# An attention and MLP kernel: lending more dead SBUF as exp outputs and shift buffers, and a second shifted copy on GpSimd

## The chip, the core and the metric

The kernel runs on one core of a Trainium2 chip. The metric is device microseconds (us) from start to end of one execution of the whole program. Engines are named as in the profile: PE (TensorE, matmuls), ACT (ScalarE), DVE (VectorE), POOL (GpSimd), SP (the queue that issues all DMAs here).

## What is computed

Two layers of pre-norm attention and an MLP with GELU, in bfloat16, on one sequence of 2048 tokens of width 512, with 32 heads of 16 and a hidden width of 1792. Both layers share their weights.

```python
def _A_ref(x, wqkv, wo):                       # x: [1, 2048, 512]
    qkv = (x @ wqkv).reshape(B, S, 3, H, Dh)   # H = 32, Dh = 16
    scores = einsum("bhqd,bhkd->bhqk", q, k) * (Dh ** -0.5)
    o = einsum("bhqk,bhkd->bhqd", softmax(scores), v)
    return o.reshape(B, S, D) @ wo
def _B_ref(x, w1, b1, w2, b2):                 # F = 1792
    return gelu(x @ w1 + b1) @ w2 + b2
for _ in range(2):
    x = x + _A_ref(layernorm(x), wqkv, wo)
    x = x + _B_ref(layernorm(x), w1, b1, w2, b2)
```

## The kernel before

**Cells.** The unit of attention is a *cell*: the scores of one head for 128 keys and 512 queries, one matmul of K = 32 rows (L1244; the queries are masked to one head by POOL, L1192, into QP). There are 4096 cells. Queries come in segments of 512 (the last one in two of 256); a *pass* is one head pair of a segment, four cells for each block of 128 keys.

**Two ways to exp.** Most cells go to ACT: groups of two or three cells lie in neighbouring PSUM banks (a *slot*), one ACTIVATE (L1601) takes the exp of the group and writes bfloat16 into places of 512 columns, the `PT` pool. Each such cell needs one matmul with V (PV, L1665), four of which run side by side on column groups of PE.
The other way is the *shift path*. DVE turns the scores into 16-bit integers whose bits, read as bfloat16, are a coarse exp (`dfirst`, L1396). Then `dchain` (L1459 on) makes three shifted copies, for a pair of cells at once: POOL adds 32 (L1473: slice 1 from slice 0), DVE adds 64 to both (L1478: slices 2 and 3 from 0 and 1, 2048 elements). PV sums the four slices with V and three scaled copies of V (`VC`, made by POOL in `vcopies`), so such a cell needs four PV matmuls. The slices lie in a *shift buffer* (`DU`), which is held from the scoring of its first cell until PV has read its last slice. Only five of the sixteen key blocks of a layer may take this path (`KD`).

**Who chooses.** All instructions are laid out ahead by a planner (`_Sched`, and `_Plan` with its generators). Each generator yields operations with costs; the planner keeps a clock for each engine, always commits the operation that can start first, and writes out the order for each engine with the semaphore waits that the data need. When a score group is committed, `attach` (L1325) may add a shift cell in a spare bank, and else `swap` (L1302) gives the third bank of the group to a shift cell, so that ACT has two cells in place of three. Both need an open pair or a free shift buffer. Constants at the head of the file set these choices; `TOL` bounds how late a bank may be, `WARM` sets when the planner adds matmuls that do nothing but keep PE busy (`fill`, L1232). `_ready` also keeps operations marked `port` (DVE's shifts) from being planned while POOL runs.

**Memory that is lent.** While parts of K of layer 1, of Q, and of V of layer 0 hold nothing, their space is given to `PT` as more places (`lent`, `lent_q`, `lend_units`; the profile then names the output kt, q or v). Beside its own 15 places and five pair buffers, the kernel before lends one more pair buffer in dead K of layer 0 once layer 0's attention is over (`morebuf`). A region is taken back when its owner needs it.

**The rest.** `post` does a segment's output projection (`wo`, L881 adds it to x), layer norm (`ln`, `ln_tile`), the h matmuls (`hpair`, L976 adds the bias into `G`), GELU on ACT (L997), the second MLP matmul (`ytile`, L1029) and the projections of layer 1 (`proj`: K and Q at L756, V at L770), spread under the attention of the next segment. Layer norm takes statistics on DVE (L666, L668), adds epsilon (L671, DVE), takes the power -1/2 on POOL (L673), makes -mean x rstd (L676, DVE) and then x x rstd + that (L689, POOL; DVE for the four first tiles and the two last). The result goes through a transposing DMA from SP (L693) into XF or XP, which the planner books with `0.3` us of SP and a tail of 3.5.

Of the kernel before, what the change touches and what calls it, by code (L numbers as in the profile page):

```python
# [5 lines left out]
ALU = mybir.AluOpType  # L6
# [7 lines left out]
H = 32  # L14
# [4 lines left out]
NL = 2  # L19
# [32 lines left out]
TOL = 0.2  # L52
# [3 lines left out]
QUEUE = 4  # L56
RUSH = 4
WINDOW = 3.4
WARM = 2.3
# [14 lines left out]
PSHIFT = 3  # L74
# [111 lines left out]
class _Op:  # L186
    __slots__ = ("eng", "cost", "fns", "reads", "writes", "sem", "by", "tail", "prio", "mode", "slack", "late", "back", "port", "limit", "after")

    def __init__(self, eng, cost, fns, reads=(), writes=(), sem=None, by=1, tail=0.0, prio=None, mode="F", slack=None):
        self.eng, self.cost = eng, cost  # L190
        self.fns = fns if isinstance(fns, list) else [fns]
        self.reads, self.writes = list(reads), list(writes)
        self.sem, self.by, self.tail, self.prio, self.mode, self.slack = sem, by, tail, prio, mode, slack
        self.limit = 1e9
        self.late, self.after = None, []
        self.port = eng == "dve" and self.writes[:1] != [] and self.writes[0].startswith(("OTT", "NMR"))
# [13 lines left out]
OWN = 0.022  # L210
HEAD = 0.14
LATENCY = {"pe": 0.2175, "act": 0.21, "dve": 0.139, "pool": 0.153328, "sp": 0.1}
OVERLAP = 0.083
# [225 lines left out]
def bass_interleave_layers__mha_block__dense_activation_gelu__prompt_kernel(  # L439
# [15 lines left out]
    with ExitStack() as es:  # L455
# [22 lines left out]
        T["PT"].append(vf[0][:, 0:8192].rearrange("p (n q) -> p n q", q=512))  # L478
# [8 lines left out]
        T["DU"].append(late.rearrange("p (i j q) -> p i j q", i=4, j=2))  # L487
        T["VC"] = sb([128, NKD, 3, H * 17], BF16, "vc")
# [15 lines left out]
        T["NMR"] = sb([128, NT], F32, "nmr")  # L504
# [37 lines left out]
SLACK = 0.3  # L542
LATE = 0.7


class _Plan:
# [12 lines left out]
    def init(self):  # L559
        T, hbm = self.T, self.hbm  # L560

        def load(dst, src, sem, keys, cost):
# [17 lines left out]
        yield ("need", ("otn", 0, (0, 0, 512), 3))  # L580
        yield _Op("pool", 1.0, lambda e: e.memset(T["V"][1][:, :, :, 16:17], 1.0),
                  writes=["V11"] + ["PART.0.%d" % g for g in range(8)])
        yield ("give", "v1ones")
# [75 lines left out]
    def ln(self, tiles, dst, dkeys, prio, quick=False, gate=None):  # L659
# [4 lines left out]
        for t in tiles:  # L664
# [6 lines left out]
        yield _Op("dve", 0.16, lambda e: e.tensor_scalar(T["VARR"][:, sl], T["MV"][:, sl, 1], 1e-5, None, op0=ALU.add),  # L671
# [4 lines left out]
        yield _Op("dve", 0.157, lambda e: e.scalar_tensor_tensor(  # L676
            out=T["NMR"][:, sl], in0=T["MV"][:, sl, 0], scalar=-1.0, in1=T["RSTD"][:, sl], op0=ALU.mult, op1=ALU.mult),
            reads=mvk + ["RSTD.%d" % c], writes=["NMR.%d" % c])
# [5 lines left out]
    def ln_tile(self, c, t, dst, dkeys, quick):  # L684
# [5 lines left out]
            T["XLN"][:, x, :], T["X"][:, t % XT, :], T["RSTD"][:, t:t + 1], T["NMR"][:, t:t + 1], op0=ALU.mult, op1=ALU.add),  # L690
            reads=["X.%d" % (t % XT), "RSTD.%d" % c, "NMR.%d" % c], writes=["XLN.%d" % x])
        if not quick:
            yield _Op("sp", 0.3, lambda e: e.dma_start(dst(t), T["XLN"][:, x, :], transpose=True),  # L693
                      reads=["XLN.%d" % x], writes=dkeys(t), sem="dtr%d" % x, by=16, tail=3.5)
            yield ("rel", "xln", x)
            yield ("give", ("lnt", t, ph))
            return
# [14 lines left out]
    def proj(self, l, kind, i, c, src, skeys, ph, done):  # L712
# [44 lines left out]
        if kind == "K":  # L757
            keys = ["K%d.%d.%d" % (l, i, c)]
            if l == 1:
                keys += ["XL.%d" % t for t in range(4 * c, 4 * c + 4)]  # L760
                if c in LEND:
                    yield ("need", ("k1", c))
# [6 lines left out]
        else:  # L769
            yield _Op("dve", DV, lambda e: e.tensor_copy(T["V"][l][:, i, :, 0:16], pb.rearrange("p (h d) -> p h d", h=H)),  # L770
# [166 lines left out]
    def wlate(self, todo):  # L937
        over = ["K0.%d.%d" % (i, c) for i in (0, 1) for c in range(self.NQ)] + ["PART1.%d" % g for g in range(4)]
        for i, (piece, (src, n), uses) in enumerate(todo):
            yield from self.wload(piece, src, n, uses, W_RING + i, over)  # L940
# [105 lines left out]
    def post(self, l, seg):  # L1046
# [20 lines left out]
        if prev:  # L1067
            yield ("need", ("gfree",) + prev)
        for p in range(NFC // 2):
# [69 lines left out]
    def setup_attention(self):  # L1139
# [18 lines left out]
        self.cap = [2] * (DU // 2) + [1] * (DU % 2) + [2]  # L1158
# [8 lines left out]
    def vcopies(self):  # L1167
        T = self.T
        for l in range(NL):
            yield ("cond", lambda l=l: self.pv >= self.lead[l])  # L1170
            for j, kt in enumerate(KD[l]):
                yield ("need", ("V", l, kt, kt // 4))
                src = T["V"][l][:, kt, :, :].rearrange("p h c -> p (h c)")
                for i, w in enumerate(VW):
                    yield _Op("pool", 0.68, lambda e, j=j, i=i, w=w, src=src: e.tensor_scalar(
                        T["VC"][:, j, i, :], src, w, 1.0, op0=ALU.mult, op1=ALU.mult),
                        reads=["V%d.%d" % (l, kt), "V%d1" % l], writes=["VC.%d.%d" % (j, i)])
# [273 lines left out]
    def over(self, du):  # L1451
        return ["K0.%d.%d" % (i, c) for i in (2, 3) for c in range(self.NQ)] if du == len(self.cap) - 1 else []

    def morebuf(self):
        yield ("cond", lambda: self.pa >= self.lead[1])
        yield ("cond", lambda: all(x == 0 for x in self.left[:self.lead[1]]))
        yield ("rel", "du", len(self.cap) - 1)

    def dchain(self, pair):  # L1459
# [22 lines left out]
        yield two  # L1482
        self.duleft[du] = n
        for jj, (pi, kt, a) in enumerate(cells):
# [30 lines left out]
    def setup_units(self):  # L1515
# [12 lines left out]
        lo = self.blocks[-1][1]  # L1528
        self.blocks.append((lo, lo + 16))
# [53 lines left out]
    def exps(self):  # L1583
        T = self.T
        u = 0
        while True:
# [17 lines left out]
            for r, (pi, kt, a) in zip(run, cells):  # L1604
# [3 lines left out]
                                         ["V%d.%d" % (l, kt), "V%d1" % l] + self.pkeys(r), ("pt", r), True, kt))  # L1608
# [100 lines left out]
    def run(self):  # L1709
# [15 lines left out]
        s.pool("du", range(len(self.cap) - 1))  # L1725
# [9 lines left out]
        s.spawn(self.morebuf(), 4)  # L1735
        s.spawn(self.lend_units(), 4)
# [36 lines left out]
```

## Time and profile before

| | |
|---|---|
| median of 3 runs | 1520.87 us (1520.8, 1520.87, 1523.39) |
| span of the profiled execution, first to last instruction | 1522.5 us; no time of its own beside the span is given |
| busy: PE, DVE, ACT, POOL | 1449.7, 1333.5, 1477.5, 823.6 us |
| cells through ACT / through the shift path | 3051 / 1045 |
| exp groups of three cells / of two | 421 / 894 |
| L1473 (POOL) / L1478 (DVE), for a pair | 1.170 / 0.744 us mean, 1.044 / 0.684 median |

The span and the runs are the same measure up to a few tenths of a per cent, so the profile's durations can be set against the median. Busy time of PE is modelled with overlapping matmuls and contains matmuls that only keep it busy, so 95% is not a full PE. A row of the profile gives busy time, mean length in ns, and the engine's idle time just before such instructions, with what ended it. Lines are those of the kernel before.

### The profile page before, as it was taken

To read this page: it belongs to the slowest core of one execution; us is meant where nothing else is said; L and a number is where in the kernel's file an instruction comes from. 1 tells how busy PE (TensorE), PEld (TensorE's weight loads), DVE (VectorE), ACT (ScalarE), POOL (GpSimd) and SP (SyncE) were. 2 spreads that over 40 slices of the span, in tenths; PEclk is the share of its full clock that TensorE was granted. 3 is DMA by queue.
4 is the path that set the end of the run, shared out by engine and by line. 5 is a ranking of instruction groups with operands and counts; after the bars stand their busy time and mean duration, and the time that the engine had idled before them with its cause. 6 is when DMAs were issued, how large, how long until landed. Compare 5 with 4: busy or idle time off the path is not lost.

```text
span 1522.5 us, 46554 instructions
## 1 busy us (share of the span) xinstructions
PE 1449.7 (95%) x20337; PEld 446.0 (29%) x20337; DVE 1333.5 (88%) x2255; ACT 1477.5 (97%) x1374; POOL 823.6 (54%) x783
## 2 busy tenths in 40 slices
PE   8998889999999999999999999899999999999998
PEld 2222222222222222222222222222222222344445
DVE  6568888989999899889989889899989999999994
ACT  7999999999999999999999999999999999999995
POOL 5425545556465554646565466556556656564550
PEclk9999999999999999999999999999999999999999
DMA  5200001144121531125221351001143115412522
GB/s 150 47 2 2 2 2 43 29 126 119 29 57 37 153 92 42 37 62 165 62 57 29 91 141 56 15 2 36 43 139 99 36 29 151 124 37 69 157 68 78
DMA packets 145046, 103.40 MB, mean 68 GB/s; under 512 B 37069, under 2 KB 143822, under 8 KB 144846
## 3 DMA queue, kind: packets, MB, share of 16 engines
q1 hardware_dynamic: 144846, 100.44, 23.4%
q8 instruction: 162, 2.65, 0.7%
q14 instruction: 38, 0.31, 0.1%
HBM read 88.61 MB, written 4.19 MB: 61 GB/s over the span
## 4 chain that ended last, share of the span: by engine, by line
ACT 58%; PE 29%; DVE 10%; issue 1%; POOL 1%; DMA 0%; ACTq 0%; DVEq 0%
ACT pt L1601 47%; PE ps L556 10%; PE ps L1244 9%; PE ps L1665 9%; ACT kt L1601 4%; DVE du L1396 4%; ACT g L997 3%; ACT v L1601 2%; DVE du L1478 2%; ACT q L1601 1%; DVE kt L1396 1%; PE ps L1232 1%; DVE g L976 1%; ACT L1601 1%; ACT L997 1%
## 5 line engine op out<-in xcount | busy, mean ns | idle before, releaser
L1601 ACT ACTIVATE pt<-ps 128x1024 bf16<-128x1024 f32 (+1 forms) x1115 | 1195.5, 1213 | 13.5 <-PE ps L1244 9.2
L1473 POOL TENSOR_SCALAR du<-du 128x1024 uint16<-128x1024 uint16 x478 | 558.6, 1170 | 482.9 <-DVE du L1396 469.3
L1396 DVE TENSOR_SCALAR du<-ps 128x512 uint16<-128x512 f32 x955 | 635.6, 683 | 82.5 <-PE ps L1244 77.6
L1244 PE MATMUL ps<-qp,kt 32*128 32x512 bf16 x4096 | 532.0, 385 | 29.9 <-ACT pt L1601 18.1
L1665 PE MATMUL ps<-pt,v 128*17 128x512 bf16 (+1 forms) x2866 | 400.6, 361 | 11.5 <-ACT pt L1601 7.9
L1665 PE MATMUL ps<-du,vc 128*17 128x512 bf16 (+1 forms) x3213 | 372.9, 359 | 5.0 <-DVE du L1478 2.0
L1478 DVE TENSOR_SCALAR du<-du 128x2048 uint16<-128x2048 uint16 x478 | 350.5, 744 | 12.0 <-POOL du L1473 11.7
L1244 PEld LDWEIGHTS ps<-qp,kt 32*128 32x128 bf16 x4096 | 137.7, 91 | 570.0 <-ACT pt L1601 191.9
L1665 PE MATMUL ps<-du,v 128*17 128x512 bf16 (+1 forms) x1071 | 178.9, 360 | 8.0 <-ACT pt L1601 2.2
L1673 PE MATMUL ps<-vc,zero 128*17 128x512 bf16 x805 | 167.0, 381 | 0.0
L556 PE MATMUL ps<-xf,wr 128*32 128x512 bf16 (+1 forms) x1888 | 129.9, 366 | 2.6 <-DMA xf<-xln 1.3
L1665 PEld LDWEIGHTS ps<-pt,v 128*17 128x17 bf16 x2866 | 98.8, 88 | 108.7 <-issue 64.8
L1665 PEld LDWEIGHTS ps<-du,vc 128*17 128x17 bf16 x3213 | 102.3, 89 | 87.7 <-issue 46.0
L556 PE MATMUL ps<-wr,g 128*32 128x512 bf16 x1600 | 117.4, 382 | 1.9 <-DVE du L1396 1.4
L1192 POOL TENSOR_SCALAR qp<-q,mask 128x512 bf16<-128x512 bf16 (+1 forms) x91 | 76.1, 837 | 63.6 <-PE ps L1244 56.5
L1601 ACT ACTIVATE kt<-ps 128x1536 bf16<-128x1536 f32 (+1 forms) x81 | 102.0, 1268 | 5.0 <-PE ps L1244 3.6
L1473 POOL TENSOR_SCALAR kt<-kt 128x1024 uint16<-128x1024 uint16 x45 | 54.6, 1214 | 75.8 <-DVE kt L1396 74.2
L1601 ACT ACTIVATE v<-ps 128x1024 bf16<-128x1024 f32 (+1 forms) x74 | 85.6, 1187 | 2.7 <-PE ps L1244 1.1
L976 DVE TENSOR_SCALAR g<-ps,hb1t 128x512 bf16<-128x512 f32 (+1 forms) x112 | 79.1, 706 | 7.3 <-PE ps L556 7.2
L1396 DVE TENSOR_SCALAR kt<-ps 128x512 uint16<-128x512 f32 x90 | 61.6, 684 | 14.0 <-PE ps L1244 12.3
L1665 PE MATMUL ps<-kt,v 128*17 128x512 bf16 (+1 forms) x314 | 71.1, 365 | 1.4 <-DVE kt L818 0.6
L1665 PEld LDWEIGHTS ps<-du,v 128*17 128x17 bf16 x1071 | 45.8, 89 | 55.0 <-issue 25.6
(90 smaller groups left out, 1242.9 us busy)
## 6 DMA issues: line engine op xcount, KB each, us to landing
wr<-in_B_w_dram SPq DMA_DIRECT2D x256, 256.0 KB, 2.9
wr<-in_A_wqkv_dram SPq DMA_DIRECT2D x24, 256.0 KB, 3.0
wr<-in_A_wo_dram SPq DMA_DIRECT2D x18, 256.0 KB, 2.9
x<-in_A_x_dram SPq DMA_DIRECT2D x7, 512.0 KB, 4.5
kept<-x SPq DMA_DIRECT2D x4, 512.0 KB, 2.9
x<-kept SPq DMA_DIRECT2D x4, 512.0 KB, 3.9
out_dram<-x SPq DMA_DIRECT2D x16, 128.0 KB, 2.8
g<-in_A_wqkv_dram SPq DMA_DIRECT2D x3, 512.0 KB, 5.9
```

The source lines that it names most:

```text
L556: return [lambda e, a=a: e.matmul(out[32 * a:32 * a + 32, :], lhsT=lhsT[:, 32 * a:32 * a + 32], rhs=rhs, start=start, stop=stop, tile_posi ...
L976: yield _Op("dve", 0.21 + n / 966, lambda e, fc=fc, pb=pb: e.tensor_scalar(T["G"][:, fc, q], pb, T["HB1T"][:, fc:fc + 1], None, op0=ALU.ad ...
L997: lambda e, g=g: e.activation(out=g, in_=g, func=ACT.Gelu_apprx_tanh), reads=gk, writes=gk, prio=2)
L1192: yield _Op("pool", 0.27 + 0.42 * w / 512, lambda e, s=s, q=q, i=i, t=t, w=w: e.tensor_scalar(T["QP"][:, s, w * i:w * i + w], q, T["MASK"] ...
L1232: fns.append(lambda e, o=o, w=w, a=a, m=m: e.matmul(o, lhsT=w, rhs=rhs, start=start, stop=start, tile_position=(0, m * a)))
L1244: return (lambda e: e.matmul(o, lhsT=lhsT, rhs=rhs, start=True, stop=True, tile_position=(32 * a, 0)), ["K%d.%d.%d" % (l, gb, kt // 4), "Q ...
L1396: yield _Op("dve", 0.682, lambda e: e.tensor_scalar(u, self.bank(b), E_SCALE, E_BIAS, op0=ALU.mult, op1=ALU.add), reads=["B.%d" % b], writ ...
L1473: one = _Op("pool", 0.15 + 0.45 * n, lambda e, a=a, b=b: e.tensor_scalar(b, a, float(SHIFT), 1.0, op0=ALU.add, op1=ALU.mult), reads=key[0] ...
L1478: two = _Op("dve", 0.152 + 0.266 * n, lambda e: e.tensor_scalar(U[:, 2:4, 0:n, :], U[:, 0:2, 0:n, :], 2 * SHIFT, None, op0=ALU.add), reads ...
L1601: yield _Op("act", 0.065 + 0.4267 * n, lambda e, src=src, dst=dst: e.activation(out=dst, in_=src, func=ACT.Exp, scale=0.25), reads=["B.%d" ...
L1665: op.fns.append(lambda e, o=o, lhsT=q[0][0][m], rhs=q[0][1][:, n * m:n * m + n], a=a, st=st, sp=sp: e.matmul(o, lhsT=lhsT, rhs=rhs, start= ...
L1673: op.fns.append(lambda e, o=self.bank(b)[32 * a:32 * a + 17, :], rhs=rhs, a=a, st=not begun[a], sp=end: e.matmul(o, lhsT=T["ZERO"][:, 0:17 ...
```

## The change

It has five parts. (1) More shift buffers in memory that is dead for a while: K of layer 1 for tokens 0 to 1023 until layer 1's K is written there, the two halves of V of layer 1, and the other half of K of layer 0 late in layer 1 (`deep_k1`, `deep_v1`, `deep_k0`); the one of `morebuf` stays. Projections of layer 1 wait until their region is returned (`k1`, `v1`), V's column of ones is set in two halves, and the late weights (`wlate`) wait for theirs. (2) `G` (14 places) and `XP` (4) are lent as exp outputs, `G` between its uses; `hpair` waits until `G` is back (`gin`). (3) In `dchain`, where POOL's clock is at most `PMORE` ahead of DVE's and `DUMORE` buffers are free, POOL makes slice 2 as well, and DVE makes only slice 3. (4) Layer norm subtracts the mean and multiplies by rstd in one operation, without `NMR`; epsilon is added on POOL. (5) The planner books a transposing DMA with 1.25 us of SP and a tail of 3.2, and several constants of its model and choices move by up to some six per cent.

```diff
 PTLOW = 5
-TOL = 0.2
+TOL = 0.192923807698
 EVAC = 0.4
...
 QUEUE = 4
+PMORE = 1
+DUMORE = 2
+GSHUT = 3
+TTAIL = 3.2
 RUSH = 4
 WINDOW = 3.4
-WARM = 2.3
+WARM = 2.17351921339
 FMARGIN = -0.1
...
 AHEAD = 24
-PSHIFT = 3
+PSHIFT = 3.095188013105
 LOG2E = 1.4426950408889634
...
         self.late, self.after = None, []
-        self.port = eng == "dve" and self.writes[:1] != [] and self.writes[0].startswith(("OTT", "NMR"))
+        self.port = eng == "dve" and self.writes[:1] != [] and self.writes[0].startswith("OTT")
 
...
 
-OWN = 0.022
-HEAD = 0.14
-LATENCY = {"pe": 0.2175, "act": 0.21, "dve": 0.139, "pool": 0.153328, "sp": 0.1}
-OVERLAP = 0.083
+OWN = 0.022265998813
+HEAD = 0.132553522424
+LATENCY = {"pe": 0.220691072014, "act": 0.210045989392, "dve": 0.140506134006, "pool": 0.158893593566, "sp": 0.103894060239}
+OVERLAP = 0.085752232862
 ROUND = 1.02
...
         T["PT"] += [T["Q"][:, :, 512 * c:512 * c + 512] for c in range(S // 512)]
-        T["PT"].append(vf[0][:, 0:8192].rearrange("p (n q) -> p n q", q=512))
+        T["PT"] += [T["G"][:, :, :], T["XP"][:, :, :], vf[0][:, 0:8192].rearrange("p (n q) -> p n q", q=512)]
         T["PART"] = [v[:, 0:8192].bitcast(F32).rearrange("p (g q) -> p g q", g=8) for v in vf[::-1]]
...
         T["DU"].append(late.rearrange("p (i j q) -> p i j q", i=4, j=2))
+        deep = [T["K"][1][:, :, 0:1024]]
+        deep[0] = deep[0].bitcast(U16).rearrange("p i (j q) -> p i j q", j=2)
+        for o in (NT * H * 17 // 2, 0):
+            deep.append(vf[1][:, o:o + 4096].bitcast(U16).rearrange("p (i j q) -> p i j q", i=4, j=2))
+        deep.append(T["K"][0][:, 0:2, :].rearrange("p c s -> p (c s)").bitcast(U16).rearrange("p (i j q) -> p i j q", i=4, j=2))
+        T["DU"] += deep
         T["VC"] = sb([128, NKD, 3, H * 17], BF16, "vc")
...
         T["RSTD"] = sb([128, NT], F32, "rstd")
-        T["NMR"] = sb([128, NT], F32, "nmr")
         PS = es.enter_context(nc.psum_tensor("ps", [128, 8 * 512], F32))
...
 FQ = 2
-SLACK = 0.3
-LATE = 0.7
+SLACK = 0.308902485584
+LATE = 0.675031221117
 
...
-        yield ("need", ("otn", 0, (0, 0, 512), 3))
-        yield _Op("pool", 1.0, lambda e: e.memset(T["V"][1][:, :, :, 16:17], 1.0),
-                  writes=["V11"] + ["PART.0.%d" % g for g in range(8)])
-        yield ("give", "v1ones")
 
...
         mvk = ["MV.%d" % t for t in tiles]
-        yield _Op("dve", 0.16, lambda e: e.tensor_scalar(T["VARR"][:, sl], T["MV"][:, sl, 1], 1e-5, None, op0=ALU.add),
+        yield _Op("pool", 0.15, lambda e: e.tensor_scalar(T["VARR"][:, sl], T["MV"][:, sl, 1], 1e-5, 1.0, op0=ALU.add, op1=ALU.mult),
                   reads=mvk, writes=["VARR.%d" % c])
...
             reads=["VARR.%d" % c, "NHALF"], writes=["RSTD.%d" % c])
-        yield _Op("dve", 0.157, lambda e: e.scalar_tensor_tensor(
-            out=T["NMR"][:, sl], in0=T["MV"][:, sl, 0], scalar=-1.0, in1=T["RSTD"][:, sl], op0=ALU.mult, op1=ALU.mult),
-            reads=mvk + ["RSTD.%d" % c], writes=["NMR.%d" % c])
         if gate:
...
         yield _Op(eng, cost, lambda e: e.tensor_scalar(
-            T["XLN"][:, x, :], T["X"][:, t % XT, :], T["RSTD"][:, t:t + 1], T["NMR"][:, t:t + 1], op0=ALU.mult, op1=ALU.add),
-            reads=["X.%d" % (t % XT), "RSTD.%d" % c, "NMR.%d" % c], writes=["XLN.%d" % x])
+            T["XLN"][:, x, :], T["X"][:, t % XT, :], T["MV"][:, t, 0:1], T["RSTD"][:, t:t + 1], op0=ALU.subtract, op1=ALU.mult),
+            reads=["X.%d" % (t % XT), "MV.%d" % t, "RSTD.%d" % c], writes=["XLN.%d" % x])
         if not quick:
-            yield _Op("sp", 0.3, lambda e: e.dma_start(dst(t), T["XLN"][:, x, :], transpose=True),
-                      reads=["XLN.%d" % x], writes=dkeys(t), sem="dtr%d" % x, by=16, tail=3.5)
+            yield _Op("sp", 1.25, lambda e: e.dma_start(dst(t), T["XLN"][:, x, :], transpose=True),
+                      reads=["XLN.%d" % x], writes=dkeys(t), sem="dtr%d" % x, by=16, tail=TTAIL)
             yield ("rel", "xln", x)
...
                 keys += ["XL.%d" % t for t in range(4 * c, 4 * c + 4)]
-                if c in LEND:
-                    yield ("need", ("k1", c))
+                yield ("need", ("k1", c))
             yield _Op(ev, DV, lambda e: copy(e, T["K"][l][:, i, cols], pb), reads=["B.%d" % b], writes=keys)
...
         else:
+            if l:
+                yield ("need", ("v1", i // 8))
             yield _Op("dve", DV, lambda e: e.tensor_copy(T["V"][l][:, i, :, 0:16], pb.rearrange("p (h d) -> p h d", h=H)),
...
     def wlate(self, todo):
+        yield ("take", ("du", self.own + 4))
         over = ["K0.%d.%d" % (i, c) for i in (0, 1) for c in range(self.NQ)] + ["PART1.%d" % g for g in range(4)]
...
             yield ("need", ("gfree",) + prev)
+        if not last:
+            yield ("need", ("gin", l, seg))
         for p in range(NFC // 2):
...
         self.dq = {k: [] for k in self.pvleft}
-        self.cap = [2] * (DU // 2) + [1] * (DU % 2) + [2]
+        self.cap = [2] * (DU // 2) + [1] * (DU % 2)
+        self.own = len(self.cap)
+        self.cap += [2] * 5
+        part = ["PART.0.%d" % g for g in range(8)]
+        self.deep = [["K0.%d.%d" % (i, c) for i in (2, 3) for c in range(self.NQ)],
+                     ["K1.%d.%d" % (i, c) for i in range(4) for c in range(2)] + ["XL.%d" % t for t in range(8)],
+                     part + ["V1.%d" % k for k in range(8, 16)], part + ["V1.%d" % k for k in range(8)],
+                     ["K0.%d.%d" % (i, c) for i in (0, 1) for c in range(self.NQ)] + ["PART1.%d" % g for g in range(4)]]
         self.lead = [min(pi for pi, p in enumerate(self.pas) if p[0] == l) for l in range(NL)]
...
     def over(self, du):
-        return ["K0.%d.%d" % (i, c) for i in (2, 3) for c in range(self.NQ)] if du == len(self.cap) - 1 else []
+        return self.deep[du - self.own] if du >= self.own else []
+
+    def vone(self, l, kt):
+        return "V11.%d" % (kt // 8) if l else "V01"
+
+    def deep_k1(self):
+        for c in range(2):
+            for kind in "KVQ":
+                for i in range(4):
+                    yield ("need", (kind, 0, 4 * c + i if kind == "V" else i, c))
+        yield ("rel", "du", self.own + 1)
+        for t in range(4):
+            yield ("need", ("xready", t, 2))
+        yield ("take", ("du", self.own + 1))
+        for c in range(2):
+            yield ("give", ("k1", c))
+
+    def deep_v1(self, half):
+        du = self.own + 3 - half
+        yield ("need", ("otn", 0, (0, 0, 512), 3))
+        yield ("rel", "du", du)
+        for t in range(8 * half, 8 * half + 4):
+            yield ("need", ("xready", t, 2))
+        yield ("take", ("du", du))
+        ks = slice(8 * half, 8 * half + 8)
+        yield _Op("pool", 1.1, lambda e: e.memset(self.T["V"][1][:, ks, :, 16:17], 1.0), writes=["V11.%d" % half] + self.over(du))
+        yield ("give", ("v1", half))
+
+    def deep_k0(self):
+        yield ("need", ("otn", 1, self.segs[1][1], (EARLY - 1) // 2))
+        yield ("rel", "du", self.own + 4)
 
...
         yield ("cond", lambda: all(x == 0 for x in self.left[:self.lead[1]]))
-        yield ("rel", "du", len(self.cap) - 1)
+        yield ("rel", "du", self.own)
 
...
         yield one
-        yield two
+        if one.eng == "pool" and self.s.clock["pool"] <= self.s.clock["dve"] + PMORE and len(self.s.pools["du"]) >= DUMORE:
+            c, d = U[:, 2, 0:n, :].rearrange("p j q -> p (j q)"), U[:, 3, 0:n, :].rearrange("p j q -> p (j q)")
+            far = _Op("dve", 0.151 + 0.134 * n, lambda e: e.tensor_scalar(U[:, 3, 0:n, :], U[:, 1, 0:n, :], 2 * SHIFT, None, op0=ALU.add),
+                      reads=key[1], writes=key[3])
+            more = _Op("pool", 0.15 + 0.45 * n, lambda e, a=a, c=c: e.tensor_scalar(c, a, float(2 * SHIFT), 1.0, op0=ALU.add, op1=ALU.mult),
+                       reads=key[0], writes=key[2])
+            far.port = more.port = True
+            yield more
+            yield far
+        else:
+            yield two
         self.duleft[du] = n
...
                 if i == 0:
-                    ws, wk = [T["V"][l][:, kt, 8 * gb + 2 * a + t, 0:17] for t in ts], ["V%d.%d" % (l, kt), "V%d1" % l]
+                    ws, wk = [T["V"][l][:, kt, 8 * gb + 2 * a + t, 0:17] for t in ts], ["V%d.%d" % (l, kt), self.vone(l, kt)]
                 else:
...
                     wk = ["VC.%d.%d" % (j, i - 1)]
+                wk = wk + self.over(du)
                 self.dq[(pi, a)].append((ws, U[:, i, jj, :].bitcast(BF16), wk + [key[i][jj]],
...
         lo = self.blocks[-1][1]
+        self.blocks.append((lo, lo + NFC))
+        for f in range(NFC):
+            self.alias[lo + f] = ["G.%d.%d" % (f, t) for t in range(4)] + ["W.%d" % i for i in range(3)]
+        lo = self.blocks[-1][1]
+        self.blocks.append((lo, lo + NDC))
+        for i in range(NDC):
+            self.alias[lo + i] = ["XP.%d" % j for j in range(4)]
+        lo = self.blocks[-1][1]
         self.blocks.append((lo, lo + 16))
...
             self.s.spawn(self.lent_q(c, *self.blocks[self.qblocks + c]), 4)
+        self.s.spawn(self.lent_g(*self.blocks[-3]), 4)
+        self.s.spawn(self.lent_xp(*self.blocks[-2]), 4)
         for gb in range(4):
...
         for u in range(*self.blocks[-1]):
+            yield ("rel", "pt", u)
+
+    def lent_g(self, lo, hi):
+        for c in range(self.NQ):
+            for kind in "KVQ":
+                for i in range(4):
+                    yield ("need", (kind, 0, 4 * c + i if kind == "V" else i, c))
+        for l in range(NL):
+            for seg in self.segs[l]:
+                self.closed.difference_update(range(lo, hi))
+                for u in range(lo, hi):
+                    yield ("rel", "pt", u)
+                yield ("need", ("otn", l, seg, GSHUT))
+                self.closed.update(range(lo, hi))
+                for u in range(lo, hi):
+                    yield ("take", ("pt", u))
+                yield ("give", ("gin", l, seg))
+                if seg[2] < 512:
+                    return
+                for t in self.tiles(seg):
+                    yield ("need", ("xready", t, 2 * l + 2))
+
+    def lent_xp(self, lo, hi):
+        for c in range(self.NQ):
+            for kind in "KVQ":
+                for i in range(4):
+                    yield ("need", (kind, 1, 4 * c + i if kind == "V" else i, c))
+        for u in range(lo, hi):
             yield ("rel", "pt", u)
...
```

The remaining lines spawn the new generators and put `self.vone(l, kt)`, the key of the right half of the ones, in the place of `"V%d1" % l`.

More of the change, by code (lines that the diff above doesn't have):

```diff
@@ L1176, in vcopies @@
                         T["VC"][:, j, i, :], src, w, 1.0, op0=ALU.mult, op1=ALU.mult),
-                        reads=["V%d.%d" % (l, kt), "V%d1" % l], writes=["VC.%d.%d" % (j, i)])
+                        reads=["V%d.%d" % (l, kt), self.vone(l, kt)], writes=["VC.%d.%d" % (j, i)])
                 yield ("give", ("vc", l, kt))
@@ L1607, in exps @@
                 self.aq[(pi, a)].append(([T["V"][l][:, kt, 8 * gb + 2 * a + t, 0:17] for t in ts], self.unit([r])[:, 0, :],
-                                         ["V%d.%d" % (l, kt), "V%d1" % l] + self.pkeys(r), ("pt", r), True, kt))
+                                         ["V%d.%d" % (l, kt), self.vone(l, kt)] + self.pkeys(r), ("pt", r), True, kt))
             yield from self.slot_done(sl)
@@ L1724, in run @@
         s.filler, s.free = self.filler, self.free
-        s.pool("du", range(len(self.cap) - 1))
+        s.pool("du", range(self.own))
         s.spawn(self.loads(), 2)
@@ L1735, in run @@
         s.spawn(self.morebuf(), 4)
+        s.spawn(self.deep_k1(), 4)
+        s.spawn(self.deep_v1(0), 4)
+        s.spawn(self.deep_v1(1), 4)
+        s.spawn(self.deep_k0(), 4)
         s.spawn(self.lend_units(), 4)
```

## The prediction

> **What bounds the kernel now.** I read the page's busy shares first, then its chain of work that ended last, then busy time by stage, then the forms of the exps inside a stage.
>
> ```profile
> PE 1449.7 (95%) x20337; PEld 446.0 (29%) x20337; DVE 1333.5 (88%) x2255; ACT 1477.5 (97%) x1374; POOL 823.6 (54%) x783
> ACT 58%; PE 29%; DVE 10%; issue 1%; POOL 1%; DMA 0%; ACTq 0%; DVEq 0%
> ```
>
> ACT is the nearest to full and carries most of the chain; POOL alone has much room. The busy time by stage (columns: length, then PE, PEld, DVE, ACT, POOL) shows that this is no mean over unlike stages:
>
> ```profile
> 215.00:380.00 165.00, 157.62 (x2044) 43.12 (x2036) 146.98 (x249) 159.70 (x150) 98.93 (x87) 0.97 0.26 73
> 380.00:700.00 320.00, 309.53 (x4127) 88.76 (x4119) 297.89 (x497) 315.11 (x300) 178.35 (x161) 1.00 0.24 67
> 700.00:900.00 200.00, 193.50 (x2564) 54.09 (x2556) 180.55 (x301) 198.76 (x190) 114.13 (x108) 1.00 0.30 84
> 1080.00:1300.00 220.00, 213.43 (x2842) 60.27 (x2838) 204.61 (x335) 216.82 (x205) 128.23 (x112) 1.00 0.30 88
> ```
>
> ACT is busy 97 to 99% everywhere, DVE 89 to 93%. So the end moves only if ACT gets less to do. ACT loses one cell of a group of three when the planner sends that cell down the shift path (DVE, POOL, DVE). What a lost cell is worth stands in the chain in order of time: exps of two cells follow each other every 4.58/5 = 0.92 us, one of three takes 1.34. So 0.43 us per cell moved.
>
> ```profile
> 120.36 1.34 ACT kt L1601
> 345.89 4.58 ACT pt L1601 x5
> ```
>
> The groups by form, from 380 to 700 us, show how many threes are left:
>
> ```profile
> L1601 ACT ACTIVATE pt<-ps 128x1024 bf16<-128x1024 f32 x199 | 190.9, 1068 | 2.7 <-PE ps L1244 2.4
> L1601 ACT ACTIVATE pt<-ps 128x1536 bf16<-128x1536 f32 x51 | 73.7, 1511 | 0.2 <-PE ps L1244 0.2
> ```
>
> With the forms that write kt and q there (the names are regions lent to exps), 68 of 292 groups are threes; and ACT idles 3 us before these, so what it waits for is nothing but its own length. Why are they threes? A pair needs a shift buffer, and there are five of two cells (a sixth after layer 0). Count cells begun against cells finished at 400 us. The first answer is the line of first operations, the second all that touches the buffers:
>
> ```profile
> 0.00:400.00 400.00, 156.68 (x233) 0.99 0.19 51
> 0.00:400.00 400.00, 110.62 (x912) 24.58 (x912) 229.02 (x348) 133.72 (x118) 0.99 0.19 51
> ```
>
> 233 cells were begun; 912 matmuls less 12 warm-up fillers are 900, at four a cell 225 finished. 8 of 10 places are taken by cells already under work, before those are added that are only scored. The buffers are close to full. The program's own plan for before (a count, no time taken) says the same: of the threes between 215 and 1480 us, 156 had no buffer free: 19 to 380 us, 43 to 700, 30 to 900, 17 to 1080, 24 to 1300, 23 to 1480.
>
> **The change, part by part.**
>
> *More shift buffers.* By the windows of the code, between about 60 and 340 us there is one more (dead K of layer 1), from 216 to 340 two more (V of layer 1), one of which stays to about 700; from about 1085 to the end there is one more (dead K of layer 0). From 700 to 1080 nothing is gained. I take back 17 of the 19 refusals to 380 us, 60% of those where one buffer is added (26 of 43, 14 of 24, 14 of 23): 71 cells. The bounds are none, if the freed place only makes pairs wait longer, and all 109 in those stages. ACT: 71 x 0.43 = 30.5 us less (0 to 47).
>
> *What that asks of DVE.* A moved cell costs half a pair: 0.683 for the first operation and half of 0.745, so 1.056; 71 of them 75 us. PE gets four quarter-rounds instead of one, 0.75 x 0.22 = 0.16 us each (in the timeline eight column matmuls take 0.61 us and four 0.39, so a round of four is 0.22), 12 us.
>
> ```profile
> L1396 DVE TENSOR_SCALAR du<-ps 128x512 uint16<-128x512 f32 x955 | 635.6, 683 | 82.5 <-PE ps L1244 77.6
> L1473 POOL TENSOR_SCALAR du<-du 128x1024 uint16<-128x1024 uint16 x478 | 558.6, 1170 | 482.9 <-DVE du L1396 469.3
> L1478 DVE TENSOR_SCALAR du<-du 128x2048 uint16<-128x2048 uint16 x478 | 350.5, 744 | 12.0 <-POOL du L1473 11.7
> ```
>
> *The second shifted copy on POOL.* Where two buffers are free and POOL is at most 1 us ahead of DVE, the 2048-element operation of DVE becomes one of 1024 on POOL (undisturbed 1.044, the median of L1473) and one of 1024 on DVE. The latter isn't in the trace undisturbed: its one instance took 0.884 behind POOL, and half of 0.684 would be 0.342. With 0.143 as what an operation of one element costs (L671 on 128x1), 0.143 + (0.684 - 0.143)/2 = 0.414; I take that. A saving of 0.27 on DVE a pair (bounds -0.2 to 0.34). How many pairs: in the plan of before both conditions hold at 17% of the pairs, the one on POOL alone at about 80%. With a buffer more for most of the time I take 34% of 523 + 35 pairs, 190: DVE 51 us less, POOL 198 us more. POOL's idle time hides them: 482.9 us of it stand before L1473, waiting for DVE. Two waits are new in such a pair: DVE's last copy stands behind POOL's second operation, and with it the first operations and copies queued on DVE (L1478 waits for POOL 12.0 us in all now); PE's matmuls of the third slice wait for POOL instead of DVE. So the buffer is held about 1 us longer.
>
> *LN.* Two small DVE operations go: L671 (25 x, 6.5 us) to POOL and L676 (25 x, 4.9 us) altogether. DVE 11 us less. On POOL the moved one is bounded by 0.14 (its DVE price) and 1.26 (the pow on the same tile); at 0.3 it is 8 us, hidden in POOL's idle 46%. The chain of an LN loses two DVE steps and one crossing: about -0.2 us where it is exposed (four tiles at the start, two at the end). I take -1 us (-2 to +2).
>
> *Transposes planned longer.* They are the same transfers: issue 1.19 to 1.23 us on SP, landing 2.4 to 4.7 us. Only the planner's order changes. PE waited for one of them 1.3 us in all, so 0 (to -3: a stretch about 247 us, where ACT idles 2.0 us and the clock is granted 0.97).
>
> *G and XP as exp outputs.* The largest group of exps has 13.5 us of idle time ahead of it in the whole span, so more places bring ACT nothing of themselves. They bring a new wait: the h groups of a segment need G back, and behind DVE's write of h (L976) its first operations would queue. The last lent places are read within one pass, 64 cells or some 23 us; the first h matmul follows the end of the segment's attention by 31 us (216.4, where the V memset starts, to 247.81). Cost 0; without that cover up to 5 us a segment. The K and V projections of layer 1 now wait with their results in a bank until a lent region is free, a buffer's hold of some ten us; nothing reads those results before layer 1, so only the bank is missed, 0 to 2 us three times, which I count at 0. The memset of V in two halves (2.34 us on POOL now) stays hidden.
>
> **Sum.** DVE: +75 - 51 - 11 = +13 us; ACT -30.5; PE +12. From 215 to 1480 us DVE idles 106 us, so it has room on the whole. It is tight in 380 to 700: 26 x 1.056 = +27, 133 pairs x 0.34 x 0.27 = -12, LN -2: 13 of 22 idle us go while the stage shrinks by 11, and DVE would run at 97 to 98%, more than any stage shows. PE at 96 to 97% has idle time and fillers in it, but also no slack for lateness. So I count three quarters: -23. With LN -24. The profiled execution's span is 1522.5; that is 1.6 above the median 1520.87, and the difference is applied to the median: **1497 us**.
>
> **Rivals.**
> 1. *Buffers were not what held the threes* (or the copies hardly ever meet their condition): the freed places are soon full again, because PV takes a pair only in its pass. Then only LN and a few cells remain, some 0 to 25 cells: 1510 to 1521. For it: PE, which must clear the pairs, is 95% busy. Against: the count of full buffers.
> 2. *More than that*: POOL takes 60% of the pairs (DVE -90) and nearly all 109 refusals go, with shorter idle of ACT: 47 + 5 to 10 us: 1460 to 1480. Against: DVE's 97% in the middle.
> 3. *Slower: DVE and POOL get in each other's way.* 245 us, the timeline:
>
> ```profile
> 246.11 0.68 DVE L1478 TENSOR_SCALAR du<-du 128x2048 uint16<-128x2048 uint16 x1
> 246.28 1.42 POOL L1473 TENSOR_SCALAR du<-du 128x1024 uint16<-128x1024 uint16 x1 [0.74 <-DVE du L1396]
> ```
>
> POOL's 1.04 becomes 1.42 when a fast DVE operation is under way; and L1478 averages 0.745 against 0.684, up to 1.54, when POOL came first. So 0.061 is lost per DVE shift now, with POOL at 54%; at random it would be 0.54 x about 0.5 = 0.27, so the planned order avoids three quarters. After, POOL is at about 71% (random 0.36) and there are some 560 such DVE operations. Each 0.1 of mean wait costs DVE 56 us; with +13 from above, DVE's 106 idle us are gone at 0.061 + 0.17 = 0.23. If the order fails and it is 0.3, DVE ends some 40 us over: 1530 to 1560. The Trainium skill ("SBUF — State Buffer", Who interferes with whom) says the two share a port pair as an exclusive lock, held for a whole instruction, whichever starts first; the trace agrees, with the last 0.14 us or so of an operation free. By that rule alone the copy trades 0.27 of DVE's lock for 1.04 of POOL's, which speaks for this rival.
>
> **Chances.** Forecast (1480 to 1510) 0.52; rival 1 0.18, a third of it within 0.2% (3 us, about what a measurement of this kernel can tell); rival 2 0.16; rival 3 0.11; 0.03 for a lent region given back late (1525 to 1535). Faster 0.52 + 0.12 + 0.16 = 0.80; same 0.06; slower 0.14. The range leaves out most of rival 3 and the far end of rival 2: 1468 to 1526.
>
> **What would show it.** Threes among L1601 fall from 421 to about 350, first operations on DVE (L1396) rise from 1045 by about 70; ACT's busy time falls by about 30; L1473 is joined by a POOL line of some 190 and a DVE line of 1024 elements near 0.42; mean of the DVE shifts stays within 0.1 of undisturbed. Wrong if the number of first operations hardly moves (rival 1), if the new DVE line averages over 0.6 or ACT waits for banks that DVE holds (rival 3).

## The result, and the profile after

The changed kernel takes 1569.82 us (1568.27 to 1573.34); before, beside it, 1520.84. The ratio is 1.0323, 95% interval 1.0308 to 1.0338: slower by 3.2%, where 1.6% faster was forecast. The profiled execution spans 1566.4 us.

First the page of the changed kernel, busy time and chain, against the two lines shown of before:

```profile
PE 1448.1 (92%) x20078; PEld 439.7 (28%) x20078; DVE 1335.1 (85%) x2213; ACT 1482.9 (95%) x1375; POOL 1018.3 (65%) x938
PE 37%; ACT 34%; DVE 16%; POOL 11%; issue 1%; DMA 1%; DVEq 0%; ACTq 0%; POOLq 0%
```

ACT has as much to do as before (1482.9 against 1477.5) and DVE too; only POOL has 195 us more. The span is 44 us longer with no more work on the engines that were full, so it is idle time that came in. And the chain that was ACT's by 58% now belongs to everyone: POOL stands in it with 11%, where it had 1%. The next view, groups of instructions by form, says with what; its last line is that of before:

```profile
L691 POOL TENSOR_SCALAR xln<-x,mv,rstd 128x512 bf16<-128x512 bf16 x58 | 129.7, 2239 | 2.3 <-DMA kt<-xln 1.0
L691 DVE TENSOR_SCALAR xln<-x,mv,rstd 128x512 bf16<-128x512 bf16 x6 | 2.5, 413 | 2.9 <-POOL rstd L678 2.9
L1529 POOL TENSOR_SCALAR du<-du 128x1024 uint16<-128x1024 uint16 x99 | 107.4, 1085 | 0.1
L1527 DVE TENSOR_SCALAR du<-du 128x1024 uint16<-128x1024 uint16 x99 | 64.0, 651 | 6.8 <-POOL du L1516 6.8
L1516 POOL TENSOR_SCALAR du<-du 128x1024 uint16<-128x1024 uint16 x408 | 467.9, 1148 | 355.5 <-DVE du L1409 345.9 <-DVE mv L673 6.8
...
L689 POOL TENSOR_SCALAR xln<-x,rstd,nmr 128x512 bf16<-128x512 bf16 x58 | 53.3, 923 | 12.1 <-DVE nmr L676 5.4 <-DMA kt<-xln 4.7 <-DMA xf<-xln 1.3
```

L691 is the layer norm's last operation, L689 of before. On POOL it took 0.923 us (53.3 us for 58) with multiply and add; with subtract and multiply it takes 2.239. On DVE the same edit changed nothing (0.413 against 0.411). The chain in order of time has 41 of the 58 in it, whole, 94 us in all, some of them in nearly every layer norm from 237 us on; two stretches of it:

```profile
237.24 4.62 POOL xln L691 x2
...
245.33 2.22 POOL xln L691
248.14 2.06 POOL xln L691
...
812.46 4.14 POOL xln L691 x2
819.76 2.49 POOL xln L691
823.26 2.54 POOL xln L691
825.82 2.42 DMA xf<-xln
828.38 1.85 PE ps L565 x16
```

What happens behind them can be seen in the timeline of the last of these stretches:

```profile
823.25 2.55 POOL L691 TENSOR_SCALAR xln<-x,mv,rstd 128x512 bf16<-128x512 bf16 x1
...
825.77 2.05 POOL L1516 TENSOR_SCALAR du<-du 128x1024 uint16<-128x1024 uint16 x2
...
826.84 1.52 DVE L1521 TENSOR_SCALAR du<-du 128x2048 uint16<-128x2048 uint16 x1 [0.91 <-POOL du L1516]
...
828.38 1.85 PE L565 MATMUL ps<-xf,wr 128*32 128x512 bf16 x16 [1.80 <-DMA xf<-xln]
...
830.82 1.02 ACT L1693 ACTIVATE pt<-ps 128x1024 bf16<-128x1024 f32 x1 [2.69 <-PE ps L1257]
```

The shift operation queued on POOL starts late, DVE waits for it (0.91), the transposing DMA lands late, PE, whose order is fixed, waits in front of the h matmuls (1.80) and makes no scores meanwhile, and then ACT, which hardly waits in before, waits for scores (2.69). Between 828 and 832 us the granted clock is 0.57 besides, so a part of this last wait is PE's slower pace. Over the span PE's wait for that DMA rises from 1.3 to 7.8 us and ACT's wait for scores ahead of its largest group from 7.1 to 37.4 (the first line of each pair is that of before; forms of 256 columns add 0.3 to the 7.5):

```profile
L556 PE MATMUL ps<-xf,wr 128*32 128x512 bf16 x1568 | 117.6, 385 | 2.5 <-DMA xf<-xln 1.3 <-DVE g L976 1.1
L565 PE MATMUL ps<-xf,wr 128*32 128x512 bf16 x1568 | 119.8, 391 | 9.6 <-DMA xf<-xln 7.5 <-DVE g L980 1.9
...
L1601 ACT ACTIVATE pt<-ps 128x1024 bf16<-128x1024 f32 x768 | 745.0, 1071 | 8.0 <-PE ps L1244 7.1
L1693 ACT ACTIVATE pt<-ps 128x1024 bf16<-128x1024 f32 x748 | 727.6, 1059 | 39.3 <-PE ps L1257 37.4
```

The stages show the same as lost busy time of ACT (columns as before):

```profile
380.00:700.00 320.00, 298.04 (x3852) 80.83 (x3848) 288.07 (x469) 303.67 (x289) 203.81 (x179) 0.98 0.20 56
700.00:900.00 200.00, 184.49 (x2394) 51.95 (x2386) 168.84 (x275) 189.55 (x176) 128.10 (x115) 0.97 0.27 78
```

Before, ACT was busy 315.11 and 198.76 us in these. The granted clock falls too. In the window 768 to 772 us, and in 248 to 252 us of before, it is 0.50; if that is the low level throughout, the mean of 0.987 is 0.013 x 2 x 1566 = 41 us spent there, against 9 for before's 0.997.

The rest of the change hardly did what was forecast. First operations of the shift path (L1409, all outputs together) are 1050 against 1045, exps of three cells 415 against 421. POOL makes the second copy for 126 of 526 pairs.

### The profile page after: what moved, and what is told of

Read it like the earlier page. It is cut to its first block, busy times and chain, and to the rows that moved or that the text cites. A ratio compares the mean times of both kernels' runs of the same rounds, so it can differ in the third digit from the quotient of the medians.

```text
span 1566.4 us, 46276 instructions
## 1 busy us (share of the span) xinstructions
PE 1448.1 (92%) x20078; PEld 439.7 (28%) x20078; DVE 1335.1 (85%) x2213; ACT 1482.9 (95%) x1375; POOL 1018.3 (65%) x938
## 4 chain that ended last, share of the span: by engine, by line
PE 37%; ACT 34%; DVE 16%; POOL 11%; issue 1%; DMA 1%; DVEq 0%; ACTq 0%; POOLq 0%
ACT pt L1693 24%; PE ps L565 13%; PE ps L1757 12%; PE ps L1257 12%; POOL xln L691 6%; DVE du L1409 6%; ACT kt L1693 3%; ACT g L1001 3%; DVE du L1521 2%; POOL du L1516 2%; DVE kt L1409 1%; ACT g L1693 1%; DVE stats L671 1%; POOL rstd L678 1%; DVE g L980 1%
## 5 line engine op out<-in xcount | busy, mean ns | idle before, releaser
L1693 ACT ACTIVATE pt<-ps 128x1024 bf16<-128x1024 f32 (+1 forms) x1063 | 1140.9, 1192 | 47.5 <-PE ps L1257 40.4
L1409 DVE TENSOR_SCALAR du<-ps 128x512 uint16<-128x512 f32 x818 | 545.2, 681 | 93.2 <-PE ps L1257 90.2
L1757 PE MATMUL ps<-du,vc 128*17 128x512 bf16 (+1 forms) x2760 | 348.9, 359 | 11.1 <-DVE du L1521 4.8
L1521 DVE TENSOR_SCALAR du<-du 128x2048 uint16<-128x2048 uint16 (+1 forms) x311 | 239.0, 779 | 12.3 <-POOL du L1516 12.3
L1516 POOL TENSOR_SCALAR kt<-kt 128x1024 uint16<-128x1024 uint16 x80 | 92.6, 1158 | 63.3 <-DVE kt L1409 62.2
L691 POOL TENSOR_SCALAR xln<-x,mv,rstd 128x512 bf16<-128x512 bf16 x58 | 129.7, 2239 | 2.3 <-DMA kt<-xln 1.0
L1409 DVE TENSOR_SCALAR kt<-ps 128x512 uint16<-128x512 f32 x160 | 108.8, 682 | 18.3 <-PE ps L1257 15.2
L1693 ACT ACTIVATE kt<-ps 128x1024 bf16<-128x1024 f32 (+1 forms) x100 | 119.2, 1213 | 5.2 <-PE ps L1257 3.4
L1757 PE MATMUL ps<-kt,v 128*17 128x512 bf16 (+1 forms) x433 | 96.4, 367 | 1.4 <-ACT pt L1693 0.6
L1757 PE MATMUL ps<-kt,vc 128*17 128x512 bf16 (+1 forms) x594 | 87.9, 342 | 0.2
```

The costliest lines, as they stand in the source:

```text
L691: yield _Op(eng, cost, lambda e: e.tensor_scalar(T["XLN"][:, x, :], T["X"][:, t % XT, :], T["MV"][:, t, 0:1], T["RSTD"][:, t:t + 1], op0=A ...
L1409: yield _Op("dve", 0.682, lambda e: e.tensor_scalar(u, self.bank(b), E_SCALE, E_BIAS, op0=ALU.mult, op1=ALU.add), reads=["B.%d" % b], writ ...
L1516: one = _Op("pool", 0.15 + 0.45 * n, lambda e, a=a, b=b: e.tensor_scalar(b, a, float(SHIFT), 1.0, op0=ALU.add, op1=ALU.mult), reads=key[0] ...
L1521: two = _Op("dve", 0.152 + 0.266 * n, lambda e: e.tensor_scalar(U[:, 2:4, 0:n, :], U[:, 0:2, 0:n, :], 2 * SHIFT, None, op0=ALU.add), reads ...
L1693: yield _Op("act", 0.065 + 0.4267 * n, lambda e, src=src, dst=dst: e.activation(out=dst, in_=src, func=ACT.Exp, scale=0.25), reads=["B.%d" ...
L1757: op.fns.append(lambda e, o=o, lhsT=q[0][0][m], rhs=q[0][1][:, n * m:n * m + n], a=a, st=st, sp=sp: e.matmul(o, lhsT=lhsT, rhs=rhs, start= ...
```

## Experiments

Two things are needed to read the expectations. The planner is part of the kernel; it books an end for the program that it lays out: 1511.4 us for before (chip span 1522.5, 11.1 more) and 1506.8 for the changed kernel (span 1566.4, 59.6 more). So the planner expected a gain of 5 us and the chip lost 44: what went wrong is something that the planner books wrongly. The 11 is no constant, though: in the runs of before beside the experiments the span is 1518.5 to 1520.1 us, 7 to 9 more than booked, and in the experiments without a subtract on POOL the distance lies between 6 and 18. And nearly any edit makes the planner lay out another order.

**1. Layer norm as before**, the rest of the change kept.

```diff
-        yield _Op("pool", 0.15, lambda e: e.tensor_scalar(T["VARR"]...
+        yield _Op("dve", 0.16, lambda e: e.tensor_scalar(T["VARR"]...
...
+        yield _Op("dve", 0.157, lambda e: e.scalar_tensor_tensor(
+            out=T["NMR"][:, sl], in0=T["MV"][:, sl, 0], scalar=-1.0, in1=T["RSTD"][:, sl], op0=ALU.mult, op1=ALU.mult),
...
-            T["XLN"]..., T["MV"][:, t, 0:1], T["RSTD"][:, t:t + 1], op0=ALU.subtract, op1=ALU.mult),
+            T["XLN"]..., T["RSTD"][:, t:t + 1], T["NMR"][:, t:t + 1], op0=ALU.mult, op1=ALU.add),
```

> The changed kernel with layer norm as before (epsilon and -mean x rstd on DVE, then x x rstd + that on POOL); all else of the change stays. Theory (POOL's subtract-then-multiply takes 2.08 us where 0.77 is planned, 58 times, and everything laid out behind it comes late): the operation is back at about 0.92 us and the time falls by most of the 49 us lost; the planner's own end for this program is 1527, and before's chip span was 11 us above its plan, so about 1538. Rival (the second copies on POOL and the lent regions cost the time): about 1570 stays.

Measured 1535.52 us, 1.0099 of before (1.0082 to 1.0116): 34 us of the 49 are gone. The operation is back at 0.96 us, the clock at 1.0. But the kernel is still 1% slower than before, and the plan said so (1527).

**2. The new layer norm alone, in the kernel before** (the reverse of that diff).

> The kernel before with the new layer norm alone (subtract, multiply on POOL, epsilon on POOL). Theory: 58 x 1.3 us late on POOL, most of it exposed: 1560 to 1580. Rival (copies and lent regions): the same as before, 1515 to 1525.

Measured 1594.02 us, 1.048 (1.0464 to 1.0495): more than expected. The span is 74 us above its plan. Copies and lent regions aren't in this kernel, so they aren't needed for the loss.

**3. Add instead of subtract**, in the changed kernel.

```diff
+        yield _Op("dve", 0.157, lambda e: e.tensor_scalar(T["NMR"][:, sl], T["MV"][:, sl, 0], -1.0, None, op0=ALU.mult),
...
-            T["XLN"]..., T["MV"][:, t, 0:1], T["RSTD"][:, t:t + 1], op0=ALU.subtract, op1=ALU.mult),
+            T["XLN"]..., T["NMR"][:, t:t + 1], T["RSTD"][:, t:t + 1], op0=ALU.add, op1=ALU.mult),
```

> The changed kernel, but DVE negates the mean (one small operation, not waiting for POOL) and POOL adds it and multiplies by rstd. If the subtract operator is what is slow, POOL's operation takes about 0.9 us, plan and chip are again some 11 us apart, and the time is about 1526 (plan 1515). If it is the order of the two steps or two scalars from SBUF with an add in front, it stays at 2.1 us and the time near 1565.

Measured 1528.95 us, 1.0054 (1.0039 to 1.0069). The group by form of this kernel:

```profile
L694 POOL TENSOR_SCALAR xln<-x,nmr,rstd 128x512 bf16<-128x512 bf16 x58 | 49.6, 860 | 4.7 <-DMA kt<-xln 2.5 <-POOL rstd L681 0.9 <-DVE du L1412 0.5
```

An add ahead of the multiply, with both scalars from SBUF, takes 0.860. So neither a first step that isn't the multiply nor two scalars from SBUF are what is slow.

**4. The planner told of the price**: `("pool", 0.77)` becomes `("pool", 2.08)`, nothing else.

> The changed kernel with only the planner's price of POOL's x - mean operation set from 0.77 to 2.08 us. Theory: the operation stays at 2.08, but the rest is laid out around it, so that the chip is again about 11 us above the plan (1530): 1541. If the 2.08 us themselves are what costs (POOL's time, not the surprise), it stays near 1565.

Measured 1551.27 us, 1.0196 (1.0181 to 1.0211), 19.5 above the plan and not 11. The operation still takes 2.20. So of the 41 us between the changed kernel and the one with the add, 18.5 come back by foresight and 22 stay while POOL is held that long. As the three orders differ, this split is no sharper than what a mere reshuffle does (runs 9 and 10).

**5. One operator changed, the order of instructions the same.** In the kernel before:

```diff
-            out=T["NMR"][:, sl], in0=T["MV"][:, sl, 0], scalar=-1.0, in1=T["RSTD"][:, sl], op0=ALU.mult, op1=ALU.mult),
+            out=T["NMR"][:, sl], in0=T["MV"][:, sl, 0], scalar=1.0, in1=T["RSTD"][:, sl], op0=ALU.mult, op1=ALU.mult),
...
-            ... T["RSTD"][:, t:t + 1], T["NMR"][:, t:t + 1], op0=ALU.mult, op1=ALU.add),
+            ... T["RSTD"][:, t:t + 1], T["NMR"][:, t:t + 1], op0=ALU.mult, op1=ALU.subtract),
```

> The kernel before, in exactly the same order of instructions, with one operator changed: L676 makes mean x rstd without the minus, and POOL and DVE subtract it after the multiply instead of adding. If subtract is what is slow on POOL, the operation goes from 0.92 to about 2.1 us and the time from 1521 to 1570 or more, though nothing else differs. If only a subtract ahead of the multiply is slow, or the mean as operand, it stays at 1521.

Measured 1575.2 us, 1.036 (1.0345 to 1.0376). From the page of this kernel, the group and the chain:

```profile
L689 POOL TENSOR_SCALAR xln<-x,rstd,nmr 128x512 bf16<-128x512 bf16 x58 | 128.2, 2213 | 8.5 <-DVE nmr L676 5.3
ACT 40%; PE 34%; DVE 15%; POOL 9%; issue 1%; DMA 1%; ACTq 0%; DVEq 0%; POOLq 0%
```

This settles it: the same operand tiles, the same order on every engine, 2.213 us in place of 0.923, and 54 us more. The 58 operations are 75 us longer together, so some seven tenths of that excess arrive at the end.

**6 to 8. The other parts taken away one at a time**, from the kernel with the add (1528.95). Without the copies on POOL:

```diff
-DUMORE = 2
+DUMORE = 99
```

> The kernel of the third run (add in place of subtract) without POOL's second copies. The prediction's step (copies free DVE, some 50 us): this should be slower than with them by 5 to 10 us. Rival (POOL and DVE block each other over the copies): faster, 1515 or less, with DVE's shift operations back at 0.745 us on the mean. Theory formed since: the copies are worth nothing that stands out of the scatter by which any edit reshuffles the laid out order: within 8 us of 1529 either way.

Without the further shift buffers (the `rel` and `take` of `deep_k1`, `deep_v1`, `deep_k0`, `wlate` left out; the other waits stay):

```diff
-        yield ("rel", "du", self.own + 1)
...
-        yield ("take", ("du", self.own + 1))
```

> The kernel of the third run without the four further shift buffers. The prediction's step (71 cells more on the shift path, 0.43 us of ACT each): slower by some 20 to 30 us, 1550 or more, and first operations on DVE fall by 70. Theory formed since (the freed places fill up again at once, since PV takes a pair only in its pass): some 20 cells fewer, and the time within 8 us of 1529.

Without G and XP as exp outputs:

```diff
-        if not last:
-            yield ("need", ("gin", l, seg))
...
-        self.s.spawn(self.lent_g(*self.blocks[-3]), 4)
-        self.s.spawn(self.lent_xp(*self.blocks[-2]), 4)
```

> The kernel of the third run without G and XP as exp outputs and without the wait for G. If the wait for G cost up to 5 us a segment, this is faster by 10 us or more. The prediction counted it at nothing, and so does the theory since: within 8 us of 1529.

| kernel | us | ratio to before | shift cells | ACT busy | DVE busy | POOL busy | planned end |
|---|---|---|---|---|---|---|---|
| before | 1520.6 to 1521.0 | 1 | 1045 | 1477.5 | 1333.5 | 823.6 | 1511.4 |
| 3: with the add | 1528.95 | 1.0054 | 1048 | 1478.4 | 1323.2 | 959.4 | 1515.3 |
| 6: no copies | 1534.79 | 1.0094 (1.0079 to 1.0109) | 1063 | 1474.9 | 1349.0 | 842.3 | 1518.0 |
| 7: no further buffers | 1534.32 | 1.0091 (1.0074 to 1.0108) | 1027 | 1486.4 | 1312.7 | 894.8 | 1520.9 |
| 8: no G, XP | 1528.08 | 1.0047 (1.0032 to 1.0062) | 1069 | 1472.6 | 1343.0 | 990.5 | 1511.8 |

Each stays within 6 us of the kernel with the add. The rival of run 6 (1515 or less without the copies) falls. The buffers bring 21 shift cells, not 71. But the sizes, and the signs too, can't be taken for the parts' worth, as the next two runs show.

**9 and 10. Only constants.** In the kernel before, eight constants of the planner moved by up to 5%, and in another the nine of the change. The work is the same but for a few cells that choose the other path (1033 and 1037 shift cells against 1045); the order is another one.

```diff
-TOL = 0.2
+TOL = 0.19189560370632106
...
-LATE = 0.7
+LATE = 0.7110648157364181
```

> The kernel before with eight constants of its planner (TOL, WARM, PSHIFT, OWN, HEAD, OVERLAP, SLACK, LATE) moved by up to 5% and nothing else: the same work in another order. Its own plan ends at 1529, that of before at 1511. Theory (the laid out order alone scatters the time, and the chip follows the plan at a distance of about 11 us): 1536 to 1542. Rival (the constants are harmless, the plan's ends mean nothing on the chip): 1518 to 1524.

> The kernel before with the nine constants of the change and nothing else (plan 1524). Theory: 1530 to 1537, by reshuffling alone. Rival (these constants fit the chip better): 1515 to 1521.

Measured 1538.95 us (1.012, 1.0104 to 1.0135) and 1533.77 (1.0087, 1.0073 to 1.0101), spans 8 above their plans in both. Nearly the same work in another order costs 18 and 13 us.

**11 and 12. Orders picked by the plan.** Of 110 draws of those constants each, for the change with the add, without and with the lending of G and XP, the one whose plan ends first (1506.7 and 1507.6).

> The change with the add in place of the subtract and without the lending of G and XP, with eight constants moved by up to 5%, those picked of 110 draws whose plan ends first (1507, before 1511). Theory: some 4 us faster than before, 1514 to 1519. Rival: the parts that are left are worth nothing on the chip, 1521 or more.

> The whole change with the add in place of the subtract, with eight constants moved by up to 5%, picked of 110 draws in the same way (plan 1508). Theory: 1515 to 1520. Rival: 1521 or more.

Measured 1525.33 (1.0027, 1.0017 to 1.0038) and 1528.02 (1.0044, 1.0031 to 1.0057). The theory fell here: the spans lie 17 above the plans, not 11, and before isn't beaten. No version was found that is faster than before.

The planner alone, without a chip, says more of the order of before. Laid out with thirty draws of the eight constants, the booked end has a median of 1518.2 us for before, 1518.3 for the change with the add and 1519.2 for that without G and XP; and before's own 1511.4 is earlier than 29 of its 30 draws. So before stands on an uncommonly good order, which nearly any edit gives up, and in the plan the parts that are left bring nothing in the middle of the draws. What they bring on the chip over many orders was not measured.

## Why the prediction was wrong, point by point

- **The step that failed first is the layer norm's: "I take -1 us (-2 to +2)".** It counted the two small DVE operations that go and never priced the operation that stays: on POOL its operators change from multiply and add to subtract and multiply. I took the length of L689 as given. It went from 0.92 to 2.24 us: 76 us of POOL in 58 pieces, each ahead of queued shift operations and of a DMA that PE waits for. The 46% of idle POOL time on the profile's page didn't cover it, because the order of all engines is laid out ahead around an operation of 0.77. With an add in the place of the subtract (run 3), 41 of the 49 us lost are gone.
- **"ACT: 71 x 0.43 = 30.5 us less" failed by its size.** There are 5 cells more, 21 between the runs with and without the further buffers. The count of full buffers was right, the conclusion wrong. Counted in the laid out orders, the refusals for want of a buffer in the stages with more buffers were to fall from 109 by 71, and are 105; between 380 and 700 us they are 43 before and 43 after, with one buffer more, while the median hold of a buffer between 400 and 600 us grew from 11.2 to 13.8 us. That is rival 1's mechanism. The same count in the orders of runs 3 and 6 to 8 shows what lengthens the hold: it is 12.5 us with all parts, 13.0 without the copies, 12.7 without G and XP, and 11.3, as in before, without the further buffers. So the added places are filled at once and a pair waits longer for PV.
- **ACT as the bound was too simple a reading.** The kernel without G and XP has 24 shift cells more than before and 5 us less on ACT, and is 0.5% slower. PE, DVE and ACT are busy 94, 88 and 96% there; that a cell taken from ACT is worth its 0.43 us only if the order lets it is my reading, no run shows it by itself.
- **The copies on POOL** took 126 pairs and not 190. The 1024-element operation on DVE has a median of 0.42 us in the kernel with the add, as estimated (0.414), but a mean of 0.59 (0.64 in the changed kernel), and the 2048-element one went from 0.745 to 0.776. So a pair saves DVE 0.13 to 0.17 and not 0.27. Rival 3's blocked time is there (0.09 us a shift of 2048 elements, 0.06 before), but it isn't what made the kernel slower: run 5 has no second copies on POOL, loses 54 us, and its shifts of 2048 elements stand at 0.07.
- **The wait for G, at 0, isn't contradicted**: without the lending the time is 0.9 us less, far within what an order scatters. The new price of the transposes wasn't tried by itself.
- **The constants were given no term at all.** Those of the change cost 13 us in the kernel before. Such a scatter, 13 and 18 us in two orders, is more than half of the gain of 24 that I forecast, and it belonged in the range.
- "Slower 0.14" was put on blocking at the port (0.11) and on a region given back late (0.03); the case that came, an operation that is slower than its form, wasn't among the cases.

What stays open: how the loss divides between the late order and the lower clock (in the profiled runs the mean granted clock is 0.978 to 0.987 in the three kernels with an unforeseen slow operation, 0.996 where the planner knows its price, 0.997 to 1.0 in all others; no run has the one without the other). An upper bound can be estimated: had PE at half clock set the pace in all of the 41 us, the clock would have cost (41 - 9)/2 = 16 of the 44 us of span, so most of the loss is the late order either way. Open, too, is what the parts that are left would bring on the chip in the mean over many orders.

## What to carry to other kernels

An operation whose operators change is a new operation, even if tile, type and engine stay: price it by its own row, and where the trace has none, say so and keep the unknown in the sum. In this program, whose order is laid out ahead, an operation that was slower than booked cost most of its excess, even on an engine that is nearly half idle. And before small gains are added up in such a program, change something that does nothing, to see how far a mere reshuffle moves the time.

## What the runs showed of the hardware

GpSimd's TENSOR_SCALAR on 128x512 bfloat16 takes 0.77 us (median) with multiply and add or with add and multiply, and 2.08 with a subtract in either place; the shortest was 2.06 to 2.07 in each of the four kernels with the subtract. VectorE takes 0.41 for all of these. In run 3 the subtract was had as an add of the negated value, for one small DVE operation more. And where a copy of 1024 elements on POOL (L1473 of before) began while a DVE shift of 2048 ran and was lengthened by it, 178 times, it ended as if it had started some 0.14 us before that shift's end.
